# Causal attention with decay and a routed expert layer: v's bound on ScalarE, the one-hot on GpSimd, fixed tiles for X, another setup, and one strict order of steps

## The chip, the cores and the metric

The kernel runs on one core of a Trainium2 chip. The metric is the device time of one execution in microseconds (us), the median of several runs. Names: TensorE (PE, with PEld for its weight loads), VectorE (DVE), ScalarE (ACT), GpSimd (POOL), SyncE (SP, which issues most transfers here).

## What is computed

Cut from the reference (B = 8, H = 8, S = 576, D = 64; N = 4608 tokens, E = 8 experts, F = 1024):

```python
scores = scale * np.matmul(q, k.transpose(0, 1, 3, 2))
log_f = np.log(np.clip(f, 0.0001, 1.0))
cum = np.cumsum(log_f, axis=-1)
scores = np.where(causal, -1e9, scores + cum[:, :, :, None] - cum[:, :, None, :])
attn = softmax(scores)
x = (attn @ v) laid out as N tokens of 512
e_idx = np.argmax(x @ w_gate + modality_bias[modality_id], axis=1)
out[mask] = gate_w[mask, None] * (np.maximum(x[mask] @ w1[e], 0.0) @ w2[e])
```

`mask` holds the tokens of expert e, and `gate_w` is the softmax weight of the chosen expert.

## The kernel before, in words

**Attention** works on 32 pairs of heads (p = 0 to 31), four pairs to a batch b. q and k of a pair lie in one tile `raw` of 128 partitions (64 per head) and 1216 columns: 576 of k, a gap of 64, 576 of q. ScalarE rounds it into the high half of X (`split_hi`, step `hi`, L373), GpSimd subtracts for the low half (`split_lo`, `lo`, L379; for pair 0 VectorE does). The pair then goes through these steps: SyncE puts the summed decay in place (`cum`); TensorE makes rough scores in three groups (`mm`), VectorE takes their maxima (`mr`, L533 to L538); the maxima are transposed on TensorE (`sp`), split on VectorE (`ssp`, L550, L551) and sent by SyncE as the shift (`so`); TensorE makes the exact scores in four groups (`s`, L578 to L593), ScalarE their exponentials (`e`, L602, L608) and rounds them to float16 (`h`, L623), GpSimd or VectorE takes the rest (`r`, L635); TensorE weights v for each of the two heads (`w`, L661 to L663), and VectorE divides (`d`, L672 to L677).

Once a batch, v is loaded (`v`), bounded, scaled and split into two float16 halves. The bound is the largest absolute value: three reductions on VectorE (`v_max`, step `vm`, L399), two transposes and small reductions (`v1`, `v3`), and a scale `sv` made from it by integer operations (`v2`, L424 to L429). ScalarE makes the high half (`vh`, L482) and the scaled gate (`gv`, L454), VectorE the low half (`vl`, L489), TensorE the keys' gate (`kg`). After a batch's last division comes its routing (`route`, steps `rt` 0 to 8, L701 to L761): maximum, index of the expert, its one-hot `oh` (L713), the one-hot times a mask of valid tokens (L716), ranks within the expert, the gate's weight (`rse`, L759 to L761), and five indirect stores of the tokens' rows (`sc`, L770) into the list of their experts, `xs`.

**What sets the order.** `steps` (L773) names each step, its engines, the steps that it follows, and the buffers that it takes and frees: 3 score buffers `ps`, one small bank `pb`, one `po`, 4 `Pt`, 2 `raw`, 3 X. `Plan.order` (L125) keeps a clock for each engine with written-down costs; it takes the ready step that could start first, a due time deciding between equals. Each engine then runs its steps in that order. `setup` (L222) runs ahead of all steps; `setup2` (L300) is a step on GpSimd.

**The expert layer** starts in the shadow of the last pairs. A list of up to 18 full tiles of 256 tokens is worked off (`full`, L1315), then half tiles of 128. A table made after six batches names the first four tiles, which hold nothing but tokens, and one made in tile 2 the others. For each tile SyncE issues the load of the next weights w1 (`load_w1`, L1110), of the tokens' rows two tiles ahead (`load_x`, L1102, a ring of three buffers `xg`) and of w2 (L1123), in the order of the code. The weights are transferred only where the expert changes. ScalarE and VectorE split the weights into two halves (L1129, L1131; L1148, L1149); TensorE does the first layer (`first`, L1185: 96 matmuls), the transposes of the next tile and the second layer (`second`, L1211); VectorE scales, and GpSimd stores the rows with two indirect transfers (L1216). What follows the last token of each expert is filled by `pads` (L1087): eight indirect writes of rows that belong to nobody, each behind a small memset (L1093, L1094). They count among the writers of `xs`, and `load_x` waits for all writers named so far. In the loop over tiles (L1334, OTHERS is tile 1) they stand ahead of all that `full` issues for the tile:

```python
            if t == OTHERS:
                pc = self.px(0)
                n = self.counts(acc, pc, "b", self.half_way)
                self.pads(pc)
            full(t)
```

Of the kernel before, what the change touches and what calls it, by code (L numbers as in the profile page):

```python
# [61 lines left out]
def f32(ap):  # L62
# [4 lines left out]
PER = 12.0  # L67
DUE = {
# [31 lines left out]
EACH = ("raw", "hi", "lo", "cum", "mm", "mr", "sp", "ssp", "so", "s", "e", "h", "r", "w", "d")  # L100


class Plan:


    TURN = 0.092
    RATE = 280e3
    LAT = {"PE": 0.22, "ACT": 0.145, "DVE": 0.12, "POOL": 0.13, "SP": 0.0}

# [3 lines left out]

    @staticmethod
    def kind(e):

        return e.rstrip("*^"), e.endswith("*"), e.endswith("^")
# [7 lines left out]
    def order(self):  # L125
        st = self.steps
        for s in st.values():
            s["after"] = [a for a in s["after"] if a in st]
        users = {}
        for s in st.values():  # L130
            for a in set(s["after"]):
                users.setdefault(a, []).append(s["name"])
        left = {n: len(set(s["after"])) for n, s in st.items()}
        done, ef, dma, rows = {}, dict.fromkeys(self.LAT, 0.0), 0.0, False
        taken = {r: [] for r in self.bufs}
        given = {}
        ready = [n for n in st if not left[n]]
        out = []
        while ready:
            best = None  # L140
            for n in ready:
                s = st[n]
                t = max((done[a] for a in s["after"]), default=0.0)
                blocked = False
                for j, (r, _) in enumerate(s["take"]):
                    k = len(taken[r]) - self.bufs[r] + j
                    if k >= 0:
                        x = given.get((r, taken[r][k]))
                        blocked = blocked or x is None
                        t = max(t, x or 0.0)  # L150
                if blocked:
                    continue
                e, port, half = self.kind(s["ops"][0][0])
                t = max(t, ef[e], ef["POOL"] if port else 0.0)
                key = (max(t, ef[e] + 0.12) + (self.TURN if e == "PE" and half != rows else 0.0), s["due"])
                if best is None or key < best[0]:
                    best = key, t, n
            assert best, ("stuck", ready, {r: v[-self.bufs[r]:] for r, v in taken.items()})
            _, t, n = best
            s = st[n]  # L160
            ready.remove(n)
            for r, x in s["take"]:
                taken[r].append(x)
            for e, d in s["ops"]:
                e, port, half = self.kind(e)
                if e == "PE" and half != rows:
                    d, rows = d + self.TURN, half
                t = max(t, ef[e], ef["POOL"] if port else 0.0) + d
                ef[e] = t
                if port:  # L170
                    ef["POOL"] = max(ef["POOL"], t)
                t += self.LAT[e]
            if s["lands"] is not None:
                dma = max(dma, t) + s["lands"] / self.RATE
                t = max(t, dma) + 2.2
            done[n] = t
            for x in s["free"]:
                given[x] = t
            out.append(s)
# [1270 lines left out]
```

## Time and profile before

| | us |
|---|---|
| median of 3 runs (860.82 to 865.59) | 862.35 |
| the profiled execution | 862.71 |
| its span, first to last instruction | 861.0 |
| TensorE busy in the span | 810.7 |
| VectorE busy | 648.2 |
| ScalarE busy | 521.4 |
| GpSimd busy | 378.2 |

The profile is that of one execution. Busy times are sums of instructions; matmuls overlap, so a busy TensorE is not TensorE at its peak. A wait names the instruction that came last before the waiting one could start. PEclk is the TensorE clock that was granted, as a share of full speed. Attention takes about the first 387 us, the expert layer the rest.

### The profile page before, as it was taken

The numbers are of one execution on the slowest core, as the hardware profiler recorded it, in microseconds if no ns is written. First come the engines' busy times: TensorE is split into PE (matmuls) and PEld (weight loads), VectorE is DVE, ScalarE is ACT, GpSimd is POOL, SyncE is SP. The second block draws the span as 40 slices with busy tenths as digits, with TensorE's granted clock in tenths as the row PEclk, the third lists the DMA queues.
The fourth block names the chain that finished last, engine by engine and source line by source line (L and its number), as shares of the span: only waits on it lengthen the run. The fifth ranks groups of instructions, "written<-read, shape, count | busy, mean of one in ns | idle before, by whom it ended". The sixth has DMA issues, their size and how long they took to land. (4 is left out here: it accounts for less than half of the span.)

```text
span 861.0 us, 23407 instructions
## 1 busy us (share of the span) xinstructions
PE 810.7 (94%) x9693; PEld 729.5 (85%) x9693; DVE 648.2 (75%) x1214; ACT 521.4 (61%) x641; POOL 378.2 (44%) x346
## 2 busy tenths in 40 slices
PE   4899999999999999889989999999999999999994
PEld 3689888888888888789979999999999999999873
DVE  7789999998989898968758766665666665666485
ACT  3577787878787878584543644545444554444384
POOL 9376788888888888686513111100101110111110
PEclk9999999999999999999999999999999999999997
DMA  5434444444444443243371840111114421105481
GB/s 191 124 121 124 128 140 141 140 153 142 153 133 151 137 156 99 71 157 140 138 267 53 339 164 34 41 46 50 37 50 147 147 65 50 50 26 202 152 300 36
DMA packets 43017, 107.49 MB, mean 125 GB/s; under 512 B 5391, under 2 KB 5583, under 8 KB 42896
## 3 DMA queue, kind: packets, MB, share of 16 engines
q1 hardware_dynamic: 36192, 84.82, 29.7%
q0 software_dynamic: 6704, 21.02, 6.5%
q8 instruction: 80, 1.31, 0.7%
q14 instruction: 41, 0.34, 0.1%
HBM read 143.14 MB, written 21.80 MB: 192 GB/s over the span
## 5 line engine op out<-in xcount | busy, mean ns | idle before, releaser
L1216 POOL DMA_INDIRECT out_dram<-y,xg x36 | 47.1, 1307 | 342.2 <-DVE y L1215 305.6
L1185 PE MATMUL ph<-xh,w1h 128*128 128x256 f32 x576 | 163.9, 285 | 4.0 <-DVE hl L1189 4.0
L1185 PE MATMUL ph<-xl,w1h 128*128 128x256 f32 x576 | 163.3, 284 | 0.0
L1185 PE MATMUL ph<-xh,w1l 128*128 128x256 f32 x576 | 163.1, 284 | 0.0
L635 POOL TENSOR_TENSOR Pl<-Pt,Ph 128x1024 f16<-128x1024 f32 (+1 forms) x63 | 141.5, 2258 | 5.7 <-ACT Ph L623 5.3
L1131 DVE TENSOR_TENSOR w1l<-raw,w1h 128x1024 fp32r<-128x1024 f32 x78 | 95.7, 1239 | 62.7 <-ACT w1h L1129 62.7
L1149 DVE TENSOR_TENSOR w2l<-raw,w2h 128x1024 fp32r<-128x1024 f32 x72 | 87.3, 1220 | 65.3 <-ACT w2h L1148 63.7
L1148 ACT CAST w2h<-raw 128x1024 fp32r<-128x1024 f32 x72 | 74.3, 1048 | 99.9 <-issue 52.9
L1129 ACT CAST w1h<-raw 128x1024 fp32r<-128x1024 f32 x80 | 82.6, 1050 | 84.8 <-PE ph L1185 59.0
L1185 PEld LDWEIGHTS ph<-xh,w1h 128*128 128x128 f32 x576 | 111.0, 193 | 5.1 <-DVE hl L1189 4.4
L379 POOL TENSOR_TENSOR X<-raw,X 128x1216 fp32r<-128x1216 f32 x31 | 85.9, 2771 | 64.2 <-ACT X L373 61.1
L1185 PEld LDWEIGHTS ph<-xl,w1h 128*128 128x128 f32 x576 | 111.0, 193 | 0.7
L1211 PE MATMUL py<-w2h,hh 128*128 128x512 f32 x288 | 111.2, 395 | 0.0
L1185 PEld LDWEIGHTS ph<-xh,w1l 128*128 128x128 f32 x576 | 110.9, 193 | 0.0
L1211 PE MATMUL py<-w2l,hh 128*128 128x512 f32 x288 | 110.0, 390 | 0.0
L1211 PE MATMUL py<-w2h,hl 128*128 128x512 f32 x288 | 109.7, 390 | 0.0
L593 PE MATMUL ps<-X 64*128 64x288 f32 (+4 forms) x1152 | 107.6, 317 | 0.0
L608 ACT ACTIVATE Pt<-ps,lnp 128x576 f32<-128x576 f32 (+1 forms) x96 | 79.5, 865 | 45.0 <-PE ps L593 45.0
L661 PE MATMUL po<-vh,Ph 128*128 128x73 f16 x930 | 100.0, 198 | 6.2 <-DVE lgh L677 3.3
L661 PEld LDWEIGHTS <-Ph 128*128 128x128 f16 x960 | 93.7, 98 | 10.3 <-DVE lgh L677 4.7
L663 PE MATMUL po<-vh,Pl 128*128 128x73 f16 x930 | 99.8, 197 | 0.3 <-DVE Pl L635 0.3
L662 PE MATMUL po<-vl,Ph 128*128 128x72 f16 x930 | 99.9, 196 | 0.0
(300 smaller groups left out, 1951.6 us busy)
## 6 DMA issues: line engine op xcount, KB each, us to landing
raw<-in_w_dram SPq DMA_DIRECT2D x84, 1024.0 KB
raw<-in_qk_dram SPq DMA_DIRECT2D x32, 608.0 KB
vT<-in_vt_dram SPq DMA_DIRECT2D x32, 320.0 KB
xg<-xs SPq DMA_DIRECT2D x18, 514.0 KB
vr<-in_v_dram SPq DMA_DIRECT2D x30, 256.0 KB
raw1b<-in_w_dram SPq DMA_DIRECT2D x4, 1024.0 KB
hxg<-xs SPq DMA_DIRECT2D x5, 257.0 KB
vr<-in_v_dram SPq DMA_DIRECT2D x8, 128.0 KB
```

The source lines that it names most:

```text
L379: e.tensor_tensor(X[:, 1], self.get("raw", p), f32(X[:, 0]), ALU.subtract)
L593: nc.tensor.matmul(ps[:, h, c0:c0 + w], X[r, x, k], X[r, y, q], start=False, stop=(j == 2), skip_group_check=True)
L608: nc.scalar.activation(self.get("Pt", (p, i))[:, :, o:o + w], ps[:, :, 0:w], AF.Exp, bias=self.lnp, scale=0.125)
L635: e.tensor_tensor(self.Pl_t[p % 2][:, :, c], self.exps(p, i), self.Ph_t[p % 2][:, :, c], ALU.subtract)
L661: nc.tensor.matmul(o, Ph[:, c0:c0 + P], vh[:, c, hh, :], start=(c == 0), stop=False)
L662: nc.tensor.matmul(o[:, 1:73], Ph[:, c0:c0 + P], vl[:, c, hh, :], start=False, stop=False)
L663: nc.tensor.matmul(o, Pl[:, c0:c0 + P], vh[:, c, hh, :], start=False, stop=(c == ic))
L1129: x = nc.scalar.copy(self.w1h[a], self.raw1[i][a])
L1131: y = e.tensor_tensor(self.w1l[a], self.raw1[i][a], f32(self.w1h[a]), ALU.subtract)
L1149: y = nc.vector.tensor_tensor(self.w2l[a], self.raw2[a], f32(self.w2h[a]), ALU.subtract)
L1185: y = nc.tensor.matmul(ph[:, i, :], w[:, k, f0:f0 + P], x[:, k, :], start=(j == 0), stop=(j == len(m) - 1))
L1211: x = nc.tensor.matmul(py, h[:, k, c * P:c * P + P], w[:, k, :], start=(j == 0), stop=(j == len(m) - 1))
```

## The change

1. v's bound is made on ScalarE: the sum of absolute values of a row's stretch of v, by an activation with an accumulator, where VectorE took the maximum. The scale that follows is made as before, from a larger bound.
2. The routing's one-hot is made on GpSimd: a table of expert numbers in which tokens that are not valid have numbers over 100, minus the index, compared with zero; the float16 one-hot is used for the ranks too. The 1e-9 of the odds is added on GpSimd.
3. X lives in three fixed tiles, whose gap is filled once in `setup`; the split reads and writes two blocks of 576 columns. `raw` has 1280 columns of room. The low split of pair 0 moves from VectorE to GpSimd.
4. `setup` fills `ones` on VectorE, makes two constants ahead of the load of f and a third behind it, rounds one part of the decay on VectorE, and splits X of the first two pairs on ScalarE ahead of the change of its tables to exponentials.
5. `Plan.order` keeps no clocks: of the ready steps whose buffers fit, it takes the one with the smallest due time. Due times are written for the first, the second, the middle and the last batch and for each pair in a batch.
6. The eight writes of empty rows are issued in tile 1 behind its `load_x` (that of tile 3), and behind both stores of tile 0.

```diff
-PER = 12.0
+PERIOD = 43.41
 DUE = {
...
+    ('vm', 0): ((-17.4022,), (-7.6216,), (-17.7721,), (-16.1893,),),
+    ('w', 0): ((36.7316, 43.5936, 56.9222, 67.6571,), (36.9699, 43.6327, 57.7499, 65.4500,), (36.2369, 44.3437, 59.2037, 65.0237,), (37.1506, 50.3202, 45.7536, 85.2972,),),
...
     def order(self):
...
+        def fits(s):
+            k = [(r, len(taken[r]) - self.bufs[r] + j) for j, (r, _) in enumerate(s["take"])]
+            return all(i < 0 or i < len(taken[r]) and (r, taken[r][i]) in given for r, i in k)
+
         while ready:
...
+            s = st[min((n for n in ready if fits(st[n])), key=lambda n: st[n]["due"])]
...
+        self.junk = self.kp.tile([P, 2, NH * D], F16, name="junk")
+        self.X3 = [self.qp.tile([P, 2, XP], F32R, name=f"X{i}", bufs=1) for i in range(3)]
...
+        for x in self.X3:
+            nc.vector.memset(f32(x[:, :, S:QC]), 0.0)
...
-        nc.scalar.copy(chl[:, 1], ft)
+        nc.vector.tensor_copy(chl[:, 1], ft)
         nc.vector.tensor_tensor(chl[:, 2], ft, chl[:, 1], ALU.subtract)
+        self.split_hi(0)
+        self.split_hi(1)
         nc.scalar.activation(one, one, AF.Exp)
...
     def split_hi(self, p):
-        X = self.new(self.qp, "X", p, [P, 2, XW], F32R, 3)
-        self.nc.scalar.copy(X[:, 0], self.get("raw", p))
+        X = self.X3[p % 3]
+        self.ring["X"] = self.ring.get("X", [])[-2:] + [p]
+        self.live["X", p] = X
+        self.nc.scalar.copy(self.two(X[:, 0]), self.two(self.get("raw", p)))
...
-        e = self.nc.gpsimd if p else self.nc.vector
-        e.tensor_tensor(X[:, 1], self.get("raw", p), f32(X[:, 0]), ALU.subtract)
+        e = self.nc.gpsimd
+        e.tensor_tensor(self.two(X[:, 1]), self.two(self.get("raw", p)), self.two(f32(X[:, 0])), ALU.subtract)
+
+    @staticmethod
+    def two(x):
+        return x.rearrange("p (a c) -> p a c", c=QC)[:, :, 0:S]
...
-        self.nc.vector.tensor_reduce(am[:, i:i + 1], self.vr[:, c], AX.XY, ALU.max, apply_absolute_value=True)
+        self.nc.scalar.activation(self.junk[:, 0:c.stop - c.start], self.vr[:, c], AF.Abs, accum_out=am[:, i:i + 1])
...
-            oh = self.new(sm, "roh", b, s3, F32, 2)
-            nc.vector.tensor_tensor(oh, self.iota_e, ei.broadcast_to(s3), ALU.is_equal)
...
-            nc.vector.tensor_tensor(oh16, self.get("roh", b), self.valid.rearrange("p (c o) -> p c o", o=1).broadcast_to(s3),
-                                    ALU.mult)
+            oh = sm.tile([P, NJ, 8], F32, name="roh")
+            nc.gpsimd.tensor_tensor(oh, self.iota_v, self.get("rei", b).broadcast_to(s3), ALU.subtract)
+            nc.gpsimd.tensor_scalar(oh16, oh, 0.0, None, ALU.is_equal)
...
-            nc.vector.tensor_scalar(se, se, 1e-9, None, ALU.add)
+            nc.gpsimd.tensor_scalar(se, se, 1e-9, None, ALU.add)
...
-            nc.gpsimd.memset(self.gap, 0)
+            x = nc.gpsimd.memset(self.gap, 0)
+            if e == 0:
+                self.order(x, self.stored)
...
+            if t == OTHERS:
+                self.pads(pc)
             behind = self.split_w2(None if t else ranks)
...
                 n = self.counts(acc, pc, "b", self.half_way)
-                self.pads(pc)
             full(t)
```

`self.stored` is the name of the last store that `second` issued.

## Rows read from the trace of the kernel before

**Rows 1.** The page, part 1: busy us, share of the span, instructions.

```profile
PE 810.7 (94%) x9693; PEld 729.5 (85%) x9693; DVE 648.2 (75%) x1214; ACT 521.4 (61%) x641; POOL 378.2 (44%) x346
```

**Rows 2.** Windows: us, busy (count) per engine, PEclk, DMA share, GB/s.

```profile
12.00:57.00 45.00, 39.72 (x536) 33.10 (x536) 35.45 (x71) 24.55 (x31) 24.72 (x23) 0.96 0.47 149
57.00:340.00 283.00, 271.19 (x5406) 243.59 (x5402) 260.08 (x620) 223.36 (x272) 227.34 (x181) 1.00 0.43 139
340.00:390.00 50.00, 44.06 (x874) 40.14 (x872) 40.25 (x113) 33.38 (x40) 37.18 (x35) 1.00 0.35 115
...
441.50:449.00 7.50, 3.50 (x18) 3.30 (x18) 5.15 (x6) 4.51 (x6) 0.00 (x0) 0.77 1.01 379
```

**Rows 3.** Timeline of ScalarE (start us, us, engine, line): two splits of X.

```profile
145.60 1.21 ACT L373 CAST X<-raw 128x1216 fp32r<-128x1216 f32 x1
...
189.93 1.21 ACT L373 CAST X<-raw 128x1216 fp32r<-128x1216 f32 x1
```

**Rows 4.** Windows, one batch of four pairs in the steady part.

```profile
145.53:189.86 44.33, 42.47 (x852) 38.07 (x849) 40.98 (x98) 34.73 (x43) 36.36 (x31) 1.00 0.44 143
```

**Rows 5.** TensorE's waits in that batch: us, times, longest.

```profile
PE ps L512 <- ACT Pt L608: 0.4, 1, 0.4
...
PE pb L724 <- DVE vl L475: 0.2, 1, 0.2
```

**Rows 6.** Timeline of GpSimd: first and last write of empty rows, and a store.

```profile
416.20 1.80 POOL L1094 DMA_INDIRECT xs<-c_nobody,c_at  x1 [0.30 <-DVE hl L1189]
...
428.83 0.97 POOL L1094 DMA_INDIRECT xs<-c_nobody,c_at  x1 [0.30 <-issue]
430.11 1.00 POOL L1216 DMA_INDIRECT out_dram<-y,xg  x1 [0.30 <-issue]
```

**Rows 7.** Timeline of SyncE: a load of tokens' rows and one of weights.

```profile
433.15 0.36 SPq L1102 DMA_DIRECT2D xg<-xs  x1
...
435.35 1.14 SPq L1110 DMA_DIRECT2D raw<-in_w_dram  x2
```

**Rows 8.** Timeline of VectorE: the low split of the weights ahead of that load.

```profile
422.91 4.63 DVE L1131 TENSOR_TENSOR w1l<-raw,w1h 128x1024 fp32r<-128x1024 f32 x4 [0.24 <-ACT w1h L1129]
```

**Rows 9.** TensorE's waits from 395 to 470 us.

```profile
PE ph L1185 <- DVE hl L1189: 4.0, 1, 4.0
```

**Rows 10.** The chain that ended last: the first layer of a tile.

```profile
461.94 11.51 PE ph L1185 x96
```

**Rows 11.** Groups by form, VectorE, that batch: busy us, mean ns | idle before.

```profile
L399 DVE TENSOR_REDUCE am<-vr 128x1 f32<-128x1024 f32 x2 | 2.4, 1204 | 0.0
...
L713 DVE TENSOR_TENSOR roh<-iota_e,rei 128x40 f32<-128x40 f32 x1 | 1.6, 1592 | 0.0
...
L399 DVE TENSOR_REDUCE am<-vr 128x1 f32<-128x512 f32 x2 | 1.3, 674 | 0.0
```

**Rows 12.** The same view, ScalarE.

```profile
L373 ACT CAST X<-raw 128x1216 fp32r<-128x1216 f32 x4 | 4.8, 1209 | 0.0
...
L482 ACT ACTIVATE vh<-vr,sv 128x1024 f16<-128x1024 f32 x2 | 2.3, 1150 | 0.0
...
L482 ACT ACTIVATE vh<-vr,sv 128x512 f16<-128x512 f32 x1 | 0.7, 716 | 0.0
...
L454 ACT ACTIVATE gv<-wg,sv 128x64 f32<-128x64 f32 x1 | 0.3, 349 | 1.0 <-DVE sv L429 1.0
```

**Rows 13.** The same view, GpSimd.

```profile
L379 POOL TENSOR_TENSOR X<-raw,X 128x1216 fp32r<-128x1216 f32 x4 | 11.1, 2770 | 6.0 <-ACT X L373 6.0
...
L707 POOL TENSOR_SCALAR rc<-rd 128x40 f32<-128x40 f32 x1 | 0.4, 368 | 0.1
```

**Rows 14.** Timeline of TensorE: the first scores.

```profile
25.11 0.34 PE L578 MATMUL ps<-later,id 64*128 64x128 bf16 x4 [0.30 <-DVE ps L535]
```

**Rows 15.** Timeline of VectorE at the start: low split of X, v's scale.

```profile
13.04 1.42 DVE L379 TENSOR_TENSOR X<-raw,X 128x1216 fp32r<-128x1216 f32 x1
...
27.93 0.15 DVE L429 TENSOR_SCALAR sv<-eb 128x1 int32<-128x1 int32 x1
```

More of the change, by code (lines that the diff above doesn't have):

```diff
@@ L127, in order @@
         for s in st.values():
-            s["after"] = [a for a in s["after"] if a in st]
+            s["after"] = {a for a in s["after"] if a in st}
         users = {}
         for s in st.values():
-            for a in set(s["after"]):
+            for a in s["after"]:
                 users.setdefault(a, []).append(s["name"])
-        left = {n: len(set(s["after"])) for n, s in st.items()}
-        done, ef, dma, rows = {}, dict.fromkeys(self.LAT, 0.0), 0.0, False
+        left = {n: len(s["after"]) for n, s in st.items()}
@@ L135, in order @@
         taken = {r: [] for r in self.bufs}
-        given = {}
+        given = set()
         ready = [n for n in st if not left[n]]
         out = []
+        def fits(s):
+            k = [(r, len(taken[r]) - self.bufs[r] + j) for j, (r, _) in enumerate(s["take"])]
+            return all(i < 0 or i < len(taken[r]) and (r, taken[r][i]) in given for r, i in k)
         while ready:
[L140 to L161, printed above, removed]
@@ L162, in order @@
+            s = st[min((n for n in ready if fits(st[n])), key=lambda n: st[n]["due"])]
+            ready.remove(s["name"])
             for r, x in s["take"]:
                 taken[r].append(x)
[L164 to L178, printed above, removed]
+            given.update(s["free"])
             out.append(s)
-            for u in users.get(n, ()):
+            for u in users.get(s["name"], ()):
                 left[u] -= 1
@@ L265, in setup @@
         nc.gpsimd.memset(self.id2, 0.0)
-        for x in range(2):
-            nc.vector.tensor_tensor(self.id2[:, x, 64 * x:64 * x + 64], self.ident[:, 0:64], self.ident[:, 64:P], ALU.add)
         def mask(t, k):
@@ L775, in steps @@
         plan = Plan(dict(ps=3, pb=1, po=1, Pt=4, raw=2, X=3, mt=2, x=2))
-        base = 0.0
         def add(name, key, eng, t, fn, args, after=(), due=0.0, **kw):
             ops = eng if isinstance(eng, list) else [(eng, t)]
-            if name in ("w", "d"):
-                kind, at = (name, key[0] % 2), key[0] // 2
-            elif name in ("ms", "mp", "mf", "mx"):
-                kind, at = (name,) + key, 0
-            else:
-                kind = (name,) + key[1:]
-                at = 0 if not key else 4 * key[0] if name in ("v", "vm", "v1", "v3", "v2", "vh", "vl", "rt", "sc", "ga", "gb", "gv", "vt", "kg", "kh", "kl") else key[0]
-            end = "a" if name in EACH and at < 2 else "z" if name in EACH and at >= n - 2 else ""
-            plan.add((name,) + key, ops, lambda: fn(*args), after, PER * at + DUE[kind + (end,) if end else kind], **kw)
-        add("setup2", (), "POOL", 8.0, self.setup2, (), due=14.0)
-        add("gs", (), [("DVE", 0.2), ("PE", 0.2), ("DVE", 0.2), ("PE", 0.2), ("DVE", 1.2)], 0, self.gate_scale, (), due=6.0, take=("pb", "gs"),
+            if not key:
+                kind, b, q = (name,) + key, 0, 0
+            elif name in ("v", "vm", "v1", "v3", "v2", "vh", "vl", "rt", "sc", "ga", "gb", "gv", "vt", "kg", "kh", "kl"):
+                kind, b, q = (name,) + key[1:], key[0], 0
+            else:
+                p, two = (key[0] // 2, (key[0] % 2,)) if name in ("w", "d") else (key[0], key[1:])
+                kind, (b, q) = (name,) + two, divmod(p, 4)
+            stage = 0 if b == 0 else 1 if b == 1 else 3 if b == nb - 1 else 2
+            plan.add((name,) + key, ops, lambda: fn(*args), after, PERIOD * b + DUE[kind][stage][q], **kw)
+        add("setup2", (), "POOL", 8.0, self.setup2, ())
+        add("gs", (), [("DVE", 0.2), ("PE", 0.2), ("DVE", 0.2), ("PE", 0.2), ("DVE", 1.2)], 0, self.gate_scale, (), take=("pb", "gs"),
             free=[("pb", "gs")])
@@ L825, in steps @@
                 u = 2 * p + h
-                add("w", (u,), "PE", 1.5, self.weighted, (u,), [("r", p, i) for i in range(3)] + [("vl", b, c) for c in range(NJ)] + [("kl", b, p % 4)],
-                    d + 19 + h, take=self.room(u))
+                add("w", (u,), "PE", 1.5, self.weighted, (u,), [("r", p, i) for i in range(3)] + [("vl", b, c) for c in range(NJ)] + [("kl", b, p % 4)], take=self.room(u))
                 add("d", (u,), "DVE", 0.99, self.divide, (u,),
-                    [("w", u), ("gb", b)] + ([("sc", b - 2, c) for c in range(NJ)] if b > 1 else []), d + 20.5 + h, free=[self.room(u)])
+                    [("w", u), ("gb", b)] + ([("sc", b - 2, c) for c in range(NJ)] if b > 1 else []), free=[self.room(u)])
         for b in range(nb):
-            d = base + PER * (4 * b) + 10
-            e = base + PER * (4 * b + 3) + 29
             k = (b,)
@@ L860, in steps @@
-                add("kh", k + (hp,), "ACT", 0.135, self.key_gate_hi, (b, hp), [("kg", b, hp), ("setup2",)], d - 5.5 + hp)
-                add("kl", k + (hp,), "DVE", 0.15, self.key_gate_lo, (b, hp), [("kh", b, hp)], d - 5 + hp, free=[("pb", ("kg", b, hp))])
-            add("ga", k, "DVE", 0.45, self.gate_sum, k, [("d", NH * b + h) for h in range(NH)], e - 1)
-            for i, ops in enumerate(([("DVE", 0.2), ("POOL", 0.25)], [("POOL", 0.5)], [("DVE", 0.4)], [("DVE", 0.45)])):
-                add("rt", k + (i,), ops, 0, self.route, (b, i), [("ga", b) if i == 0 else ("rt", b, i - 1)], e + i)
+                add("kg", k + (hp,), "PE", 1.1, self.key_gate, (b, hp), [("vt", b, hp), ("gv", b), ("kg",) + divmod(4 * b + hp - 1, 4) if b or hp else None] + free, take=("pb", ("kg", b, hp)))
@@ new lines, in steps @@
+                add("kh", k + (hp,), "ACT", 0.135, self.key_gate_hi, (b, hp), [("kg", b, hp), ("setup2",)])
+                add("kl", k + (hp,), "DVE", 0.15, self.key_gate_lo, (b, hp), [("kh", b, hp)], free=[("pb", ("kg", b, hp))])
+            add("ga", k, "DVE", 0.45, self.gate_sum, k, [("d", NH * b + h) for h in range(NH)])
+            for i, ops in enumerate(([("DVE", 0.2), ("POOL", 0.25)], [("POOL", 0.68)], [("DVE", 0.2)], [("POOL", 0.65), ("DVE", 0.23)])):
+                add("rt", k + (i,), ops, 0, self.route, (b, i), [("ga", b) if i == 0 else ("rt", b, i - 1)])
@@ L872, in steps @@
+            add("rt", k + (6,), "POOL", 0.25, self.route, (b, 6), [("rt", b, 5), ("rt", b, 8), ea])
             for c in range(NJ):
-                add("sc", k + (c,), "POOL", 1.12, self.scatter, (b, c), [("sc", b, c - 1) if c and b < nb - 1 else ("rt", b, 6)], e + 8 + c, lands=263e3)
+                add("sc", k + (c,), "POOL", 1.12, self.scatter, (b, c), [("sc", b, c - 1) if c and b < nb - 1 else ("rt", b, 6)], lands=263e3)
         if early:
-            add("early", (), [("PE", 0.2), ("DVE", 4.0), ("POOL", 4.0)], 0, early, (), [("sc", EB, c) for c in range(NJ)],
-                base + PER * (4 * EB + 3) + 40, take=("pb", "e"), free=[("pb", "e")])
+            add("early", (), [("PE", 0.2), ("POOL", 0.15), ("DVE", 4.5), ("SP", 2.3)], 0, early, (), [("sc", EB, c) for c in range(NJ)], take=("pb", "e"), free=[("pb", "e")])
```

162 lines of the change are left out of this document (106 added, 56 removed), and 54 rows, old and new, of the table DUE.

## The prediction

> **What bounds the kernel now.** I began with the engines' busy shares: TensorE is busy 94% of the 861.0 us span, VectorE 75%, ScalarE 61%, GpSimd less [rows 1]. TensorE's work is not changed, so only its idle and its slow time can be won. The windows by stage say where that lies [rows 2]: 45.0 - 39.72 = 5.3 us idle from 12 to 57 us, 283.0 - 271.19 = 11.8 us in the steady part of attention, 50.0 - 44.06 = 5.9 us in its tail, and one hole of 4 us at 441.5 us in the expert stage. The change reaches no more than these, plus the first 12 us and the slow clock.
>
> The steady part is strictly periodic: the split of X for one head pair starts at 145.60 us and that of the pair four later at 189.93 us [rows 3], so a batch of four pairs takes 44.33 us. In that window TensorE is busy for 42.47 us, VectorE for 40.98, ScalarE for 34.73 and GpSimd for 36.36 [rows 4]. TensorE loses 44.33 - 42.47 = 1.86 us, in six waits. The longest, 0.4 us, ends on ScalarE; the other five (0.2 to 0.3 us) all end on VectorE [rows 5] (the first and the last of the six). VectorE, 92% full, is the engine that is late, but each wait is short and TensorE is nearly full. No saving on another engine can be worth over 1.86 us a batch, or 11.8 us over the stretch.
>
> **The change part by part.** The sum is made against the profiled execution's 862.71 us (span 861.0 and 1.7 around it), which stands 0.36 above the median of 862.35.
>
> *The empty rows behind the load.* GpSimd issues eight writes of empty rows from 416.20 us on; the last starts at 428.83, and only then, at 430.11, the second store of the first tile's output [rows 6]. SyncE's load of the fourth tile's rows waits for that store's buffer and for the eight writes, and issues at 433.15; behind it on the same queue stands the load of the next first-layer weights, at 435.35 [rows 7]. VectorE had freed those weights' buffer at 422.91 + 4.63 = 427.5 us [rows 8]. The weights land late, and TensorE waits 4.0 us for a VectorE step that stands behind their split [rows 9]. Over 441.5 to 449 us the granted clock is 0.77 of full, a mix of its levels of 1.2 and 2.4 GHz after the hole, and 18 matmuls take 7.5 us [rows 2]. At full clock 96 of them take 11.51 [rows 10], so 18 take 2.16, and the hole costs 5.3 us. After the change the store takes the place of the first write, at 416.2, and the load, which issued 3.0 us after it, can go at 419.3; behind it the weights' load can go at 427.5, 7.9 us earlier than now. The hole needs 5.3, so it closes. What is late next is TensorE itself. The eight writes move back by one place in the queue, 430.11 - 428.83 = 1.3 us, and the load that needs them comes a tile later, so that costs nothing. Bounds: 0 (another thing holds the weights) to -5.3. I take **-5.3**, since the slack covers it.
>
> *The bound of v on ScalarE.* VectorE loses per batch 2 x 1.204 + 0.674 us of reductions (the second form's two include one of the next batch) = 3.08 us [rows 11]. ScalarE gains three passes over the same elements. No row shows an absolute value with an accumulated sum; the nearest are the scalings of v from the same tile, 2 x 1.150 + 0.716 = 3.02 us [rows 12]. The upper bound is this and a small activation of 0.35 us behind each to bring out the sum (the scaled gate in [rows 12]), so 4.1 us; the lower is 3.02. I take 3.02, the row with the same tile, shape and engine. ScalarE then stands at about 37.5 of 44.33 us.
> The Trainium skill (ScalarE: Activation LUTs, Rules for kernel authors) speaks against this: it gives simple elementwise work and maxima to VectorE, up to about three times faster in bf16. An estimate by that rule, three times 3.08, is 9.2 us a batch: ScalarE at 43.7 of 44.33 would be a second bound and the steady gain below would be nothing, 853 in all. The trace differs for this tile in float32: 1.204 us on VectorE, 1.150 on ScalarE.
>
> *The one-hot on GpSimd.* VectorE loses one comparison of 40 elements that takes 1.592 us here [rows 11], and the product behind it. GpSimd gains a subtraction and a comparison, and one more small step for the sum of the odds; a step of this size takes it 0.368 us [rows 13], so 1.1 us at 36.36 of 44.33, beside TensorE's work. Routing leads to the scatter, on which TensorE waits nowhere in the steady part, so I cost it at nothing; uncovered it would be 1.1 us a batch.
>
> *X without its gap.* The split reads 1152 columns, not 1216: 1.209 to 1.15 us on ScalarE [rows 12], 2.770 to 2.62 on GpSimd [rows 13], four times a batch. Both stand beside TensorE; with the one-hot, GpSimd's sum is about even (+1.1 - 0.6).
>
> *The strict order.* It sets the order in every queue anew, and nothing in a trace of before shows its waits. VectorE goes from 40.98 to about 36 us a batch, so the five waits that end on it (1.4 of the 1.86 us) can go. TensorE's switches between half- and full-row matmuls do not become fewer in the new list, so its busy time stays. Bounds over the 283 us: -11.8 (all waits gone) to 0, and above 0 only by the rival below. Between the ends I take the half, **-5.9**: most waits name the engine that is relieved, but an order with fixed places leaves some of its own.
>
> *The start.* Ahead of the first scores, at 25.11 us [rows 14], VectorE makes the shift of the first pair, and its queue holds the first low split (1.42 us) and one of v's reductions; ahead of v's scale, at 27.93 [rows 15], it holds that split and all three reductions. They leave VectorE: 1.42 + 1.20 = 2.6 us ahead of the scores and 1.42 + 3.08 = 4.5 ahead of the scale. Against it, one more reduction of the second pair comes ahead of the first shift (I price it at 0.67, v's reduction of the nearest size), and GpSimd does the first low split, 2.6 us, ahead of the rest of its setup, so that all later low splits come that much later. The three small fills of X and the rounding that comes over from ScalarE add to VectorE while it waits for loads, and I take nothing for them; nor for the splits of X ahead of the table load, since the first shift is held by VectorE. Bounds: -8 (the 5.3 us idle of the stage, and as much again as half of it in slow clock: 0.96 is granted over the 45 us [rows 2]) to +2.6 (GpSimd's delay on the path). I take **-3**, between the 2.6 - 0.67 = 1.9 and the 4.5 of the two chains.
>
> *The tail.* 5.9 us are idle there in an order that changes wholly; bounds -5.9 to +5.9, and I take **-1**, a sixth of it, since the end has less work left to fill a wait with.
>
> Sum: 862.71 - 5.3 - 5.9 - 3 - 1 = 847.5; less the 0.36 to the median, **847**.
>
> **The rivals.**
> *The order wins nothing in the steady part.* For it: TensorE is 96% busy and a fixed order makes waits of its own; against: the waits name VectorE. Then the start and the empty rows alone count, 862.35 - 5.3 - 3 = 854.
> *The hole stays.* If the weights' load is held by its place in the queue or VectorE's order again puts the split ahead of the step that TensorE needs, 847 + 5.3 = 852. Against it: 7.9 us of slack.
> *Nearly all idle goes.* 862.35 - 5.3 - 11.8 - 8 - 4 = 833, with most of the tail's 5.9. Against it: six waits in a batch, and each must go.
> *Slower: ScalarE's queue.* The three passes stand in the same queue as the exponentials that free the score buffers. ScalarE is idle for 44.33 - 34.73 = 9.6 us a batch, but in many gaps, so a pass of 1.15 can push an exponential, and with it TensorE. Uncovered they cost 8 x 3.02 = 24 us; half of it is 12, and 862.35 + 12 - 5.3 = 869. It decides when over 5.3 / 8 = 0.66 us a batch is uncovered. For it speaks the one wait that ends on ScalarE; against it the 6.8 us a batch that stay free.
> The Trainium skill (ScalarE: Activation LUTs, Table sets) says that the absolute value is in every table set, by which no table load would be added; no run here shows it.
>
> **How the numbers follow.** Half a per cent, 4.3 us, is about what a measurement of this kernel tells from no change. Chances: the forecast 0.50 (its own range 841 to 851), nothing in the steady part 0.20, the hole stays 0.10, nearly all idle goes 0.10, slower 0.07, and 0.03 for a loss at the start or in the tail that takes the rest back to about 860. The range goes from 837 to 858: it leaves out the slower case, the 0.03 and half of the best case. Faster by over 0.5% (under 858.0) holds in all but the last two and a part of the second rival: 0.86; same 0.07; slower 0.07.
>
> **What would show it.** The period between splits of X four pairs apart: 43.4 us is right, 44.3 is the first rival, over 45 the slower one, with exponentials as what ended TensorE's waits. The load of the fourth tile's rows issues near 420 us, no wait of over 1 us stands on TensorE before the last half tiles, and the granted clock there does not fall. The first scores begin near 23 us. If the passes over v take over 1.5 us, or VectorE stays at 41 us a batch, the reasons are wrong even where the time is right.

## The result: 1.6% faster, and the profile after

| | before | after |
|---|---|---|
| median, us | 862.06 (860.82 to 865.59, 4 runs) | 848.75 (846.39 to 849.61, 4 runs) |
| ratio | | 0.9843, 95% interval 0.9809 to 0.9876 |
| the profiled execution, us | 862.71 | 849.61 |
| its span, us | 861.0 | 847.8 |

Forecast was 847. The total came out, but three of its four terms were off: the steady part won more than was forecast, the start won nothing and the tail lost. That these nearly cancel is luck; the table of stretches below has the sizes. Single executions of one kernel lie up to 10 us apart here, and with them the clock that TensorE is granted in the mean (0.991 in the execution of 841.9 us of e12 below, 0.980 in that of 851.5), so kernels are compared by medians and their details by traces.

The page of the kernel after, part 1, which answers to [rows 1]: VectorE is down from 648.2 to 627.7 us, ScalarE up from 521.4 to 543.2.

```profile
PE 807.1 (95%) x9693; PEld 726.9 (86%) x9693; DVE 627.7 (74%) x1170; ACT 543.2 (64%) x688; POOL 378.7 (45%) x370
```

The windows by stage, for [rows 2]; the last is the stretch that held the hole, 8.6 us earlier, since the expert layer begins so much earlier (first matmul at 377.2 us, not 385.8).

```profile
12.00:57.00 45.00, 39.04 (x540) 32.43 (x541) 32.58 (x72) 29.34 (x42) 25.82 (x28) 0.85 0.40 131
57.00:340.00 283.00, 280.59 (x5638) 253.15 (x5634) 245.87 (x611) 245.99 (x317) 238.02 (x210) 1.00 0.44 143
340.00:390.00 50.00, 42.06 (x714) 38.41 (x711) 37.54 (x94) 31.29 (x38) 30.02 (x39) 0.93 0.38 131
432.00:440.00 8.00, 8.00 (x58) 7.52 (x58) 5.89 (x9) 4.30 (x7) 1.74 (x1) 1.00 0.88 256
```

In the steady part TensorE's idle went from 11.8 to 2.4 us, and the hole is gone. The start and the tail did not get better: 6.0 and 7.9 us are idle where it was 5.3 and 5.9, and the clock is lower in both.

One batch, for [rows 4], its splits of X on ScalarE, for [rows 3], and TensorE's waits in it, for [rows 5]:

```profile
141.42:183.64 42.22, 41.91 (x847) 37.79 (x846) 36.38 (x91) 37.25 (x49) 36.47 (x31) 1.00 0.47 150
```

```profile
141.44 1.16 ACT L397 CAST X<-raw 128x1152 fp32r<-128x1152 f32 x1
...
183.66 1.16 ACT L397 CAST X<-raw 128x1152 fp32r<-128x1152 f32 x1
```

```profile
PE po L689 <- DVE lgh L705: 0.3, 1, 0.3
```

The period is 42.22 us, not 44.33. Of six waits one is left.

**Where the 13.2 us of span went.** Four marks cut the traces: VectorE's first division of an attention head, its 56th of 64, the first matmul of the expert layer, and the end. Timeline of VectorE, before:

```profile
47.77 0.20 DVE L672 TENSOR_SCALAR z<-po,sv 128x5 f32<-128x5 f32 x1
...
348.91 0.21 DVE L672 TENSOR_SCALAR z<-po,sv 128x5 f32<-128x5 f32 x1
```

and after:

```profile
47.95 0.22 DVE L700 TENSOR_SCALAR z<-po,sv 128x5 f32<-128x5 f32 x1 [0.33 <-PE po L691]
...
335.14 0.23 DVE L700 TENSOR_SCALAR z<-po,sv 128x5 f32<-128x5 f32 x1 [0.34 <-PE po L691]
```

| stretch, us | before | after | difference | forecast | after, again (e11 below) |
|---|---|---|---|---|---|
| to the first division | 47.8 | 48.0 | +0.2 | -3 | 44.1 |
| to the 56th | 301.1 | 287.2 | -14.0 | -5.9 | 289.0 |
| to the first expert matmul | 36.9 | 42.1 | +5.2 | -1 | 43.3 |
| to the end | 475.2 | 470.6 | -4.6 | -5.3 | 470.8 |

The last column is a second profile of the kernel after, in another execution. Its start is 3.9 us shorter, at a higher clock. Its steady part is 1.8 us longer at the full clock, which is not explained here.

### The profile page after: what moved, and what is told of

It is laid out like the page before. It is cut to its first block, busy times and chain, and to the rows that moved or that the text cites. A ratio compares the mean times of both kernels' runs of the same rounds, so it can differ in the third digit from the quotient of the medians.

```text
span 847.8 us, 23444 instructions
## 1 busy us (share of the span) xinstructions
PE 807.1 (95%) x9693; PEld 726.9 (86%) x9693; DVE 627.7 (74%) x1170; ACT 543.2 (64%) x688; POOL 378.7 (45%) x370
## 4 chain that ended last, share of the span: by engine, by line
PE 86%; DVE 7%; POOL 2%; issue 2%; ACT 1%; DMA 0%; DVEq 0%; POOLq 0%; ACTq 0%
PE ph L1211 23%; PE py L1237 23%; PE ps L621 9%; PE pb L491 4%; PE po L689 4%; PE po L691 3%; PE po L690 3%; PE ps L551 3%; PE ps L613 3%; PE ps L546 2%; PE ph L1293 2%; PE ps L606 2%; PE px L1194 2%; PE ps L540 2%; DVE w1l L1157 1%
## 5 line engine op out<-in xcount | busy, mean ns | idle before, releaser
L1157 DVE TENSOR_TENSOR w1l<-raw,w1h 128x1024 fp32r<-128x1024 f32 x78 | 97.6, 1265 | 61.5 <-ACT w1h L1155 61.5
L621 PE MATMUL ps<-X 64*128 64x288 f32 (+4 forms) x1152 | 109.8, 319 | 0.0
L403 POOL TENSOR_TENSOR X<-raw,X 128x1152 fp32r<-128x1152 f32 x32 | 84.7, 2649 | 38.5 <-ACT X L397 38.2
L636 ACT ACTIVATE Pt<-ps,lnp 128x576 f32<-128x576 f32 (+1 forms) x96 | 81.3, 864 | 24.9 <-PE ps L621 24.9
```

What stands on the lines that cost most here:

```text
L403: e.tensor_tensor(self.two(X[:, 1]), self.two(self.get("raw", p)), self.two(f32(X[:, 0])), ALU.subtract)
L621: nc.tensor.matmul(ps[:, h, c0:c0 + w], X[r, x, k], X[r, y, q], start=False, stop=(j == 2), skip_group_check=True)
L636: nc.scalar.activation(self.get("Pt", (p, i))[:, :, o:o + w], ps[:, :, 0:w], AF.Exp, bias=self.lnp, scale=0.125)
L1157: y = e.tensor_tensor(self.w1l[a], self.raw1[i][a], f32(self.w1h[a]), ALU.subtract)
```

## The experiments

Medians with the ratio to the kernel before and its 95% interval; 4 to 8 runs each.

| | us | ratio |
|---|---|---|
| e1 after, table of tiles later | 849.33 | 0.9852 (0.9824 to 0.9880) |
| e2 after, first low split behind the setup | 845.40 | 0.9821 (0.9797 to 0.9845) |
| e3 after, empty rows ahead again | 851.47 | 0.9892 (0.9868 to 0.9917) |
| e4 after, v's bound and one-hot back on VectorE | 865.14 | 1.0031 (1.0004 to 1.0058) |
| e5 before, with v's bound on ScalarE, one-hot on GpSimd | 885.81 | 1.0253 (1.0214 to 1.0292) |
| e6 before, with the empty rows behind the load | 858.29 | 0.9934 (0.9909 to 0.9959) |
| e7 after, one-hot back on VectorE | 856.36 | 0.9896 (0.9849 to 0.9943) |
| e8 e2, table of tiles later still | 848.99 | 0.9811 (0.9769 to 0.9853) |
| e9 before, with v's bound on ScalarE | 871.56 | 1.0093 (1.0060 to 1.0127) |
| e10 e2, table of tiles in four pieces | 850.25 | 0.9857 (0.9828 to 0.9886) |
| e11 after, again | 850.90 | 0.9869 (0.9843 to 0.9895) |
| e12 e2, again, beside e11 | 847.19 | 0.9809 (0.9773 to 0.9845) |

### Relief or order: e4, e5, e9, e7

**e4**, the strict order without the relief:

```diff
-        self.nc.scalar.activation(self.junk[:, 0:c.stop - c.start], self.vr[:, c], AF.Abs, accum_out=am[:, i:i + 1])
+        self.nc.vector.tensor_reduce(am[:, i:i + 1], self.vr[:, c], AX.XY, ALU.max, apply_absolute_value=True)
...
-            nc.gpsimd.tensor_tensor(oh, self.iota_v, self.get("rei", b).broadcast_to(s3), ALU.subtract)
-            nc.gpsimd.tensor_scalar(oh16, oh, 0.0, None, ALU.is_equal)
+            nc.vector.tensor_tensor(oh, self.iota_e, ei.broadcast_to(s3), ALU.is_equal)
+            nc.vector.tensor_tensor(oh16, self.get("roh", b), self.valid.rearrange("p (c o) -> p c o", o=1).broadcast_to(s3),
+                                    ALU.mult)
```

> The kernel after, with v's bound (a maximum) and the one-hot back on VectorE, in the strict order as it is. Theory (VectorE's relief is what takes the waits away): the period of four pairs, 42.2 us after, goes to 43.5 to 44.5, VectorE is busy for about 41 us of it, waits on VectorE come back, and the time is 858 to 864. Rival (the order alone does it): the period stays under 42.8 and the time is 848 to 852.

Measured: 865.14 us, 16 over the kernel after and even above the kernel before. A batch takes 44.66 us, and TensorE's waits in it all end on VectorE:

```profile
PE ps L609 <- DVE mt L564: 1.3, 1, 1.3
PE po L692 <- DVE lgh L708: 0.6, 2, 0.4
PE pb L755 <- DVE vl L506: 0.4, 1, 0.4
```

The order alone, with the new setup and the fixed tiles, wins nothing, though this kernel has the better place of the empty rows.

**e5** is the other half: the same moves (e4's diff, reversed, with the ranks too made from the float16 one-hot) in the kernel before, the order of its steps unchanged.

> The kernel before, order of steps unchanged, with only v's bound on ScalarE, the one-hot on GpSimd and the 1e-9 on GpSimd. Theory (relief and order are worth something together only: the order without relief was 16 us slower than with it, and 3 us slower than before): some of the waits on VectorE go, the period of four pairs falls from 44.33 to between 43.2 and 44.0, and the time is 851 to 860. Rival A (relief alone does it all): the period is under 42.8 and the time 848 to 851. Rival B (in the old order ScalarE's three passes push the exponentials): the period stays at 44.3 or grows, waits on ScalarE come, and the time is 861 or more.

Measured: 885.81 us, 22 slower than before; a batch takes 47.86 us, at a granted clock of 0.96:

```profile
141.60:189.46 47.86, 44.13 (x852) 39.48 (x849) 36.95 (x93) 37.11 (x48) 37.05 (x34) 0.96 0.42 133
```

Against [rows 4] TensorE's idle grew by 1.9 us a batch, and the same 852 matmuls take 1.7 us more at the lower clock. Rival B's time and period came true, and further than written, but its mechanism did not: TensorE's wait for an exponential is 0.3 us there, and it was 0.4 [rows 5]. New on ScalarE is one wait of 0.3 us, for a pass over v itself. The timelines of VectorE and of GpSimd in e5 show one of its waits, once a batch:

```profile
188.64 0.23 DVE L719 TENSOR_REDUCE rtot<-roh 128x8 f32<-128x40 f16 x1 [2.27 <-POOL roh L717]
188.78 0.23 DVE L476 TENSOR_TENSOR vl<-pb,vh 128x80 f16<-128x80 f32 x1
```

```profile
185.22 2.77 POOL L380 TENSOR_TENSOR X<-raw,X 128x1216 fp32r<-128x1216 f32 x1 [2.60 <-ACT X L374]
187.95 0.25 POOL L716 TENSOR_TENSOR roh<-iota_v,rei 128x40 f32<-128x40 f32 x1
188.28 0.32 POOL L717 TENSOR_SCALAR roh<-roh 128x40 f16<-128x40 f32 x1
```

GpSimd waits 2.60 us for ScalarE's split of X, then does its own split, and only behind it the one-hot, 0.57 us of work. VectorE, whose queue is in order, stands still for 2.27 us, and behind it stands the step that frees the small bank of TensorE:

```profile
PE pb L724 <- DVE vl L476: 1.7, 1, 1.7
```

VectorE is busy for only 36.95 of 47.86 us there: relieved, and later than ever. The other small waits of the batch are like those of before.

**e9** is e5 without the one-hot.

> The kernel before, order of steps unchanged, with only v's bound on ScalarE. Theory (the 22 us that both reliefs cost in the old order come from the one-hot: GpSimd does it behind a 2.77 us split of X, and VectorE, whose queue is in order, waits 2.3 us for it a batch): no such wait here, the period stays between 43.6 and 44.6, and the time is 857 to 866. Rival (ScalarE's three passes push X's split and the exponentials, which is the slower rival of the prediction): the period is over 46 and the time over 875.

Measured: 871.56, between the two. So of the 22 us some 9 come from v's bound and the other 14 from the one-hot. From 125 us on the period is 45.7 us, and 47.1 in the one batch (from 171 us) where the granted clock is 0.96 and not 1.00. The rank matmul waits 1.1 or 1.2 us for VectorE where it was 0.2 [rows 5]. What ScalarE's pass over v makes late is a split of X. Timelines of ScalarE and of VectorE in e9:

```profile
181.50 1.05 ACT L400 ACTIVATE junk<-vr 128x1024 f16<-128x1024 f32 x1
...
183.43 1.22 ACT L374 CAST X<-raw 128x1216 fp32r<-128x1216 f32 x1
```

```profile
185.75 1.80 DVE L717 TENSOR_TENSOR roh<-roh,valid 128x40 f16<-128x40 f32 x1
```

The pass stands ahead of that split, which starts 2.95 us behind the exponential before it, where it was 2.03. GpSimd, which waits 2.92 us for it, does the low half from 184.72 to 187.49 us. VectorE's product of the one-hot and its mask is held until then: it takes 1.80 us, where the kernel before has 0.38 at this place. Behind it in VectorE's queue stands the step that TensorE waits for. VectorE has lost three reductions and is still busy for 40.7 us of a batch (40.98 before).

**e7**, in the new order, puts the one-hot, its mask and the 1e-9 back.

> The kernel after, with only the one-hot, its mask and the 1e-9 back on VectorE; v's bound stays on ScalarE. Theory (v's 3.08 us a batch is the larger part of the relief, the one-hot's 1.6 to 1.8 the smaller): the period goes from 42.25 to 42.6 to 43.2, the time to 851 to 855. Rival (the one-hot is the part that counts, since it stalls VectorE while GpSimd works and stands ahead of a divide): period over 43.5, time 857 or more. Third: nothing, 847 to 850, since VectorE has room left.

Measured: 856.36, and a period of 44.02: 1.8 us of the 2.1 that a batch had won are lost again. (By the medians it is 5.5 to 7.6 us in all, less than such batches add up to; that was not taken apart.) Of the one-hot's two steps the comparison takes 1.592 us in the kernel before [rows 11]; here it is the product with the mask that takes 1.611:

```profile
L747 DVE TENSOR_TENSOR roh<-roh,valid 128x40 f16<-128x40 f32 x1 | 1.6, 1611 | 0.0
...
L744 DVE TENSOR_TENSOR roh<-iota_e,rei 128x40 f32<-128x40 f32 x1 | 0.2, 201 | 0.0
```

In most batches the 1e-9, 0.17 us in the kernel before, is long here too:

```profile
182.87 1.25 DVE L791 TENSOR_SCALAR rse<-rse 128x5 f32<-128x5 f32 x1
```

The same kind of step takes about 0.2 us when nothing is in its way. These steps are long here because they are held up, not because they are large, and with them the larger part of the gain goes: the theory (v's bound is the larger part) fell. Being held is not the whole price: in e4 the mask product takes 0.56 us, and the batch is longer still. How the 1.8 us divide among them was not run apart. Nor was v's bound alone put back in the new order; with the one-hot already back it costs another 0.6 us a batch (44.66 in e4, 44.02 here).

### The empty rows: e6, e3

**e6** moves `self.pads(pc)` in the kernel before as the change does, nothing else.

> The kernel before, with only the eight writes of empty rows moved behind the tile's load and behind the stores of tile 0. Theory (the hole of the kernel before is 5.3 us with its slow clock, and this place closes it): 855 to 858, with no wait over 1 us on TensorE in that tile. Rival (as in the kernel after, where putting them back cost 1.2 us of waits in the profiled execution and 2.7 by the medians): 859 to 861, and a part of the wait stays.

Measured: 858.29, and a span of 856.1, 4.9 under that of before with attention unchanged. The window of the hole, for the fourth row of [rows 2], and TensorE's waits from 395 to 470 us, for [rows 9]:

```profile
441.50:449.00 7.50, 7.33 (x49) 6.55 (x49) 6.78 (x11) 4.36 (x7) 0.57 (x1) 1.00 1.01 244
```

```profile
PE ph L1187 <- DVE hl L1191: 0.2, 1, 0.2
```

**e3** takes that move out of the kernel after.

> The kernel after, with the eight writes of empty rows back ahead of the tile's loads. Theory (that place alone makes the hole): TensorE waits 4 us once in the third tile and 848.8 becomes 853 to 855 (+5.3 by the prediction's sum). Rival (the hole needed more than that place, such as the old order's end or the weights' split): no wait over 1 us, 848 to 850.

Measured: 851.47, against 848.75 and 850.90 for the kernel after, so 0.6 to 2.7 more. In its profile the hole is there, but small:

```profile
PE ph L1209 <- DVE hl L1213: 1.5, 2, 1.2
```

From the first expert matmul to the end e3 takes 471.8 us, the kernel after 470.6 and 470.8. The place is worth 4.9 us under the old order and 1.0 to 1.2 under the new one. Why the same queue holds TensorE less there was not found out.

### The start: e2, e11, e12

In the kernel after GpSimd does pair 0's low split at 10.23 us, ahead of its second setup, and TensorE's first matmul waits for a fill of that setup until 13.72. Timelines of GpSimd, VectorE and TensorE, after:

```profile
10.23 2.99 POOL L403 TENSOR_TENSOR X<-raw,X 128x1152 fp32r<-128x1152 f32 x1
```

```profile
10.68 2.75 DVE L307 TENSOR_TENSOR id<-ident 128x64 bf16<-128x64 f32 x2
```

```profile
13.72 0.37 PE L467 MATMUL pb<-ident,gmax 128*1 128x128 f32 x1 [13.72 <-POOL vh L329]
```

**e2** does the split behind the setup, by one due time:

```diff
-    ('lo',): ((-30.4199, -46.7722, 10.3081, -40.1680,),
+    ('lo',): ((-7.5000, -46.7722, 10.3081, -40.1680,),
```

> The kernel after, with one due time changed: GpSimd does the low split of pair 0 behind its second setup instead of ahead of it. Theory (that split, 2.99 us, holds up GpSimd's setup on which TensorE's first work waits, and draws out VectorE's id2 step from some 0.2 us to 2.75): TensorE starts near 11 us instead of 13.7, and the first divide comes 2 to 3 us earlier than 47.95; the time is 845 to 847. Rival (the start is held by v's chain and the transfers that feed it): TensorE starts earlier, waits longer behind it, and the time stays at 848 to 850. Third: the split is now late for the first exact scores and the time is 850 or more.

Measured: 845.40. VectorE and TensorE in e2:

```profile
10.69 0.34 DVE L307 TENSOR_TENSOR id<-ident 128x64 bf16<-128x64 f32 x2
```

```profile
11.31 0.37 PE L467 MATMUL pb<-ident,gmax 128*1 128x128 f32 x1 [11.31 <-DVE gmax L465]
```

The same step on VectorE takes 0.34 us, not 2.75, TensorE begins 2.4 us earlier, and the first division comes at 41.64 us. But the clock differed too: 0.96 from 12 to 57 us, where the profiled execution of the kernel after has 0.85. So both were run again side by side.

> The kernel after, unchanged, beside the next one on the same chip. Both theories: 847 to 850, the first divide at about 44 us where TensorE's granted clock from 12 to 57 us is 0.96 and at about 48 us where it is 0.85.

> The kernel after with pair 0's low split behind GpSimd's second setup, again, to set its gain against the kernel after on one chip. Theory (the split costs 2.4 us of the start at either clock: the first divide came at 41.64 against 44.08, and at 45.50 against 47.95): 2 to 3 us under the kernel after, 844.5 to 847.5, with the lowest run under 844.5. Rival (845.4 was a draw of executions with the faster start): within 1 us of the kernel after.

Measured: 850.90 and 847.19, a gain of 3.7 where 2 to 3 was expected (over all runs of either, 10 each, the medians are 849.3 and 846.0). The first division against the clock from 12 to 57 us:

| | clock 0.96 | clock 0.85 |
|---|---|---|
| after | 44.09 (e11) | 47.95 |
| split behind the setup | 41.64 (e2) | 45.57 (e12) |
| difference | 2.4 | 2.4 |

The split costs 2.4 us at either clock, and the clock 3.9 with either split. e2's kernel has the lowest medians of this study, 1.8 to 1.9% under before.

### The tail: e1, e8, e10

In the kernel after TensorE stands for 5.0 us at 345 us. VectorE works there through the 25 small steps of the table of the first tiles (`early`), and only behind them does the rest of pair 29 that frees a score buffer. Timelines of VectorE, of GpSimd and of TensorE, after:

```profile
341.79 2.53 DVE L1026 TENSOR_TENSOR c_lea<-c_cuma,c_io 1x32 f32<-1x32 f32 x1
...
346.32 2.32 DVE L1072 TENSOR_SCALAR c_done<-c_done 1x8 f32<-1x8 f32 x1
...
348.95 1.23 DVE L663 TENSOR_TENSOR Pl<-ps,Ph 128x1024 f16<-128x1024 f32 x1
```

```profile
341.65 2.63 POOL L403 TENSOR_TENSOR X<-raw,X 128x1152 fp32r<-128x1152 f32 x1
346.27 2.36 POOL L663 TENSOR_TENSOR Pl<-Pt,Ph 128x1152 f16<-128x1152 f32 x1 [1.99 <-ACT Ph L651]
```

```profile
350.23 0.50 PE L606 MATMUL ps<-later,id 64*128 64x128 bf16 x8 [4.98 <-DVE Pl L663]
```

Two steps of 32 and 8 elements take 2.53 and 2.32 us, each until a step of GpSimd ends. **e1** makes the table due at 336.0 instead of 334.4029:

> The kernel after, with one due time changed: the table of the first four expert tiles (`early`) at 336.0 instead of 334.40, so that VectorE and GpSimd do the rest of pair 29 ahead of its 29 tiny steps. Theory (the tail lost its time there): TensorE's wait of 5.0 us on VectorE at about 345 us goes or falls under 2 us, the last divide comes 4 to 6 us earlier, and the time is 843 to 846. Rival (the end is bound by the chain of the last pairs, whatever stands ahead of it): the wait only moves, the last divide stays within 1 us, and the time is 848 to 850. A third way: the table is now late for the expert layer, whose first matmul comes later, 850 or more.

**e8** at 340.3, on top of e2:

> The kernel after, with pair 0's low split behind GpSimd's second setup, and the early table due at 340.3, behind the shift of pair 30 instead of ahead of the rest of pair 29. Theory (VectorE's chain for the table belongs where TensorE has other work; moved by one step it only moved the wait): the wait of 5 us in the tail falls to under 2, the granted clock there stays near 1.00, and the time is 838 to 843. Rival (the chain holds the one small bank's next user wherever it stands): a wait of 4 to 6 us under another name, 844 to 847.

**e10** cuts it into four steps, on top of e2:

```diff
-    ('early',): ((334.4029,),),
+    ('early',): ((335.0,),), ('early2',): ((341.2,),), ('early3',): ((342.9,),), ('early4',): ((352.0,),),
```

> The kernel after, with pair 0's low split behind GpSimd's second setup, and the early table cut into four steps, due at 335.0 (4 steps of VectorE), 341.2 (10), 342.9 (7, and the two loads of rows) and 352.0 (4), with work of the last pairs between them. Theory (as one block of 25 steps that VectorE must end before it does anything for TensorE the chain costs one wait of 5 us wherever it stands; in pieces the waits are covered): no wait of over 2 us in the tail, the granted clock there near 1.00, and the time 837 to 842. Rival (the tail has too little work for TensorE, and the waits add up to the same): 843 to 847.

Measured: 849.33, 848.99 and 850.25, none faster, clear of the noise, than the kernel that it was made from. From 340 to 390 us the granted clock is 0.93, 0.93 and 0.90, where it is 0.93 in the kernel after; the theories of e8 and e10 had it near 1.00. The wait only changes its name. In e1:

```profile
PE pb L572 <- DVE rtot L746: 5.7, 1, 5.7
```

in e8:

```profile
PE po L689 <- DVE lgh L705: 4.9, 1, 4.9
```

and in e10, in more pieces:

```profile
PE po L691 <- POOL between L796: 3.5, 1, 3.5
PE po L691 <- DVE Pl L663: 1.7, 1, 1.7
```

The theory that the table's place makes the loss fell three times. What is shown is that with the table elsewhere another wait of 3.5 to 5.7 us takes the place of this one; why, and what would shorten the tail, stays open.

e4 says whose loss it is. With VectorE's relief off its steady part wins nothing (300.6 us to the 56th division), and yet its tail takes 42.8 us, like the 42.1 of the kernel after, with the same longest wait:

```profile
PE ps L609 <- DVE Pl L666: 5.2, 1, 5.2
```

So the loss comes with the strict order. Of the 5.2 us TensorE's idle makes 2.7 (5.6 us between the marks before, 8.3 after). The rest, 2.4, is the same work at a lower clock: 0.92 is granted between the marks after, behind the wait of 5 us, and 1.00 before.

## Why the prediction was right in the total and wrong in its terms

**Empty rows behind the load: right.** -5.3 was taken; the expert stage is 4.6 shorter, and the move alone gives 4.9 of span in e6. The load of the fourth tile's rows issues at 412.83 us; with the 8.6 by which the expert layer begins earlier that is 421.4 on the old scale, where 419.3 was forecast, and no wait of over 0.2 us is left from 395 to 470 us. (The slack forecast as 7.9 us is 435.35 - 427.54 = 7.8; that changes nothing.)

**The strict order: the mis-sized term.** The forecast put -5.9 on the stretch, half of its bound of 11.8. Its idle fell by 9.4, and by the marks -14.0 was won, -12.1 in e11 (301.1 us are 6.8 batches, and 6.8 x 2.11 = 14.3). Two steps failed. Half of the idle was taken because "an order with fixed places leaves some of its own": one wait of 0.3 us was left. And the bound itself was too low. "No saving on another engine can be worth over 1.86 us a batch", yet a batch fell by 2.11: TensorE's busy time fell too, from 42.45 to 41.9 us for the same matmuls. The forecast had its busy time stay. Counted over four batches, 8 gaps of a batch became 1, so each gap that went also took 0.08 us of busy time with it (0.56 / 7). I read that as the end of a matmul that shows only where nothing follows; it was not measured apart. The order alone does not do it: in e4, in the same order but with its waits back, the batch has 42.37 us busy.

**The two moves off VectorE: costed one by one, and apart from the order.** The sums were right: VectorE at 36.38 us a batch (some 36 forecast), and ScalarE at 37.25 (37.5). The passes over v take 2 x 1.059 + 0.619 and three small reads of the sum of 0.198, 3.3 us, inside the bounds of 3.02 to 4.1:

```profile
L427 ACT ACTIVATE junk<-vr 128x1024 f16<-128x1024 f32 x2 | 2.1, 1059 | 0.0
...
L427 ACT ACTIVATE junk<-vr 128x512 f16<-128x512 f32 x1 | 0.6, 619 | 0.0
L427 ACT ACTIVATION_READ_ACCUMULATOR junk<-vr 128x1 f32 x3 | 0.6, 198 | 0.0
```

The Trainium skill (ScalarE: Activation LUTs, Table sets) holds here: both traces have two table loads, of 1.283 us each, so the absolute value brought none. But the one-hot and the 1e-9, taken as nothing on GpSimd, are worth 1.8 of the 2.1 us a batch (e7). What they remove from VectorE are steps of 0.2 us that GpSimd's long steps stretch to as much as 1.6, ahead of steps that TensorE waits for.

**The slower rival was real, in another kernel and by another way.** In the old order the passes cost 9 us and the one-hot on GpSimd 14 more. But it is not that "a pass of 1.15 can push an exponential, and with it TensorE": TensorE's wait for an exponential did not grow in e5 or e9. A pass pushed a split of X, GpSimd's half of the split came later, and VectorE was held behind it. The rival was given 0.07 for the 6.8 us a batch that ScalarE keeps free, which is an argument from sums. What kept it away was the new order, which the forecast had priced as a small gain of its own.

**X without its gap: right.** 1.156 and 2.633 us where 1.15 and 2.62 were worked out. What the fixed tiles are worth in time was not run by itself; e4 has them and wins nothing.

**The start: the size at like clock, by one chain of the two.** -3 was taken for work that leaves VectorE, and +0.2 was measured. The first exact scores came at 27.25 us, not near 23, and later than the 25.11 of before [rows 14]; v's scale, the other chain, came at 25.46 us, 2.5 earlier than before [rows 15], where the forecast had up to 4.5. Timelines of TensorE and of VectorE, after:

```profile
27.25 0.38 PE L606 MATMUL ps<-later,id 64*128 64x128 bf16 x4
```

```profile
25.46 0.15 DVE L457 TENSOR_SCALAR sv<-eb 128x1 int32<-128x1 int32 x1
```

"GpSimd does the first low split, 2.6 us, ahead of the rest of its setup" was seen, but priced as a delay of later splits; it holds TensorE's first matmul (2.4 us, e2) and a step of VectorE. At the higher clock, e11, the first division comes 3.7 us before that of the kernel before, where TensorE is granted 0.96 from 12 to 57 us in both. So a gain is there, and the profiled execution lost it to 3.9 us of slow clock. How much of it v's scale makes was not run apart.

**The tail: wrong in sign.** -1 was taken, from a bound of 5.9 either way; +5.2 was measured, 2.7 of it idle and 2.4 slow clock. That "the end has less work left to fill a wait with" is a reason for a loss, and it was put beside a gain. A lower clock behind a long wait, which the forecast had priced in the hole of the expert stage, was not priced here. That the loss comes with the order is shown by e4; why the order does it stays open.

## What to carry to other kernels

Moving work off the fullest engine and changing the order of the queues are one change: here either alone made the kernel slower or no faster (+22 us, and +3), and both together made it 13 faster. So don't discard a move after trying it in the old order, and don't argue from sums of busy time when the queues are in order: look at what stands ahead of the moved step and who waits behind it. A small step with eight times its usual duration is, here, a wait that the profile counts as work, and the first thing to move.

## What was not expected of the hardware

**A small step on VectorE can be held until a step on GpSimd ends.** The step that makes `id2` takes 2.75 us beside a split of 2.99 us on GpSimd and 0.34 without it; two steps of the table take 2.53 and 2.32 us and end with GpSimd's. VectorE counts as busy meanwhile. The Trainium skill (SBUF — State Buffer, Who interferes with whom) says that a VectorE instruction with two inputs in SBUF, against a GpSimd instruction that reads SBUF, or a VectorE copy or `tensor_scalar` in one of its fast modes, contends with GpSimd for a shared pair of ports, and that the second to come is blocked until the first ends. All three cases agree with it, though no trace shows in which mode a `tensor_scalar` ran. The held steps of e7 agree too: the 1.61 us of the mask product end 0.06 us behind GpSimd's step, so 1.4 us of its price were never VectorE's work.

**The clock of the start falls for longer in some executions than in others.** In two executions of the same kernel TensorE is busy for 5.6 of the 8 us from 12 us on, at a granted clock of 1.00; of the 6 us from 20 us on it is busy for 3.4 in the one and 3.9 in the other, and there the clock falls in both. Windows of the kernel after in its first profile, and in e11:

```profile
20.00:26.00 6.00, 3.41 (x33) 2.15 (x33) 4.55 (x14) 1.10 (x3) 4.29 (x2) 0.76 0.18 63
26.00:32.00 6.00, 6.00 (x52) 5.14 (x52) 4.79 (x8) 3.53 (x5) 0.00 (x0) 0.50 0.57 211
```

```profile
20.00:26.00 6.00, 3.87 (x43) 2.66 (x41) 4.60 (x14) 1.28 (x3) 4.32 (x2) 0.89 0.16 49
26.00:32.00 6.00, 6.00 (x81) 5.16 (x77) 5.38 (x10) 4.45 (x6) 0.00 (x0) 0.82 0.77 271
```

In the first the lower level (0.50, 1.2 GHz) holds through the next 6 us, in which 52 matmuls run instead of 81. The first division comes 3.9 us later there, more than any edit at the start in this study moved it. What makes it hold longer in one execution is open.
